# First layer, first MLP product: ten of fourteen tiles in five pairs, each pair as seven products of quarters

## The chip, the cores and the metric

The kernel runs on one core of one Trainium2 chip, in one launch. The metric is the device time of one execution in microseconds. An execution is a little longer than the span from its first to its last instruction, which the profile's times count from.

## What is computed

A vector `x` of 2048 tokens by 640 channels goes through two rounds of a spectral layer (A: a filter between a 2D FFT and its inverse) and a token-mixing MLP (B). B works across the tokens, for each channel alone:

```python
def _B_ref(x, w1, b1, w2, b2):
    h = _layernorm(x, axis=-1)                  # (B, S, D), S = 2048, D = 640
    u = jnp.einsum("bsd,sf->bdf", h, w1) + b1   # F = 1728
    u = _gelu(u)
    y = jnp.einsum("bdf,fs->bds", u, w2) + b2
    return (lambda x, *d: x.transpose(*d))(y, 0, 2, 1)   # (B, S, D)

x = x + _A_ref(_layernorm(x), A_w_r, A_w_i)
x = x + _B_ref(_layernorm(x), B_w1, B_b1, B_w2, B_b2)
x = x + _A_ref(_layernorm(x), A_w_r, A_w_i)
x = x + _B_ref(_layernorm(x), B_w1, B_b1, B_w2, B_b2)
```

The change concerns the einsum with `w1` in the first round.

## The kernel before

**Stages.** `run` calls, for each round, `a1` and `a2` (the spectral layer; `a2` ends with the normalised input `hf` of the MLP, 16 row blocks j of 128 tokens by 640 channels in f32) and then the MLP: `b1st` in the first round, `b2nd` in the second.

**Precision.** Every factor is split into a high and a low f16 part and a product is three matmuls (`mm3`): high x high, high x low, low x high. `hh` (or `hha` for rows 0 to 7, written already in `a2`) and `hl` are the parts of `hf`. Weights are scaled by a power of two first: `scan1` sums squares of a raw tile on ACT, `scale1` adds them on DVE, sums over the partitions by a one-column matmul with `ones` on PE, and takes the power on DVE in six small steps; `step(m)` advances this by one stage. `wload` fetches the raw f32 tile in two halves, `wsplit` makes the high part on ACT and the low part on DVE.

**The first product.** The 1728 columns of `w1` are 14 tiles of 128, the last one doubled to fill it (tile 13, whose two halves are added up afterwards). `SEQ` orders them in pairs t, t+7: 6, 13, 0, 7, 1, 8 and so on. A tile takes 16 row blocks x 3 terms x 2 halves of 320 channels, 96 matmuls (64 for tile 13). The first two tiles share the start: `both_high` runs their high parts against the rows that are there, the last four rows later, then `rest` adds the low rows. Each later tile is `both`, with the next tile's split and the scans of later tiles at fixed row blocks beside it. A gelu on ACT follows each tile; the split of its result into `uh` and `ul`, the factors of the second product, stands at the end.

**For the second round.** That round computes its first product by quarters: a pair of tiles is a 2 x 2 matrix of quarters A11 to A22 (first index the tile, second the half of the rows), `hf` one of B11 to B22, and seven products of sums (S1 to S4 of A, T1 to T4 of B) of 8 row blocks each take the place of eight. The first round forms the parts for it beside its own work and writes them to DRAM: `wstore` writes the split tiles, `wsum` forms S1 to S4 in buffers of their own, `wssplit` splits and writes them (pair 5's as f32 sums). All of these writes are issued by POOL.

**Order.** The tile framework orders instructions by readiness, except where `self.pin` is on: then `Pin` ties each instruction behind the one written before it on its engine. In `b1st` the pin is off for the copies of `hf` to `hh` (rows 8 to 15), on for the forming of `hl`, and off again for all that follows until the last three tiles. `a2` is pinned as a whole. DMA issues on SP go past `Pin`.

**The second product** (16 tiles of `w2`, 84 or fewer matmuls each, in the order of `SEQ`) follows at once, with its own splits and scans, and ends with the first steps of the second round's spectral layer. Its buffers (`a0_open`) lie where `h` and its neighbours were.

Of the kernel before, what the change touches and what calls it, by code (L numbers as in the profile page):

```python
# [3 lines left out]

# [6 lines left out]
F32 = mybir.dt.float32  # L11
# [41 lines left out]
SEQ = [t + 7 * i for t in (6, 0, 1, 2, 3, 4, 5) for i in range(2)]  # L53
# [34 lines left out]
class Layers:  # L88
# [41 lines left out]
    def setup(self):  # L130
# [16 lines left out]
        self.qt = base.tile([128, NFT], F32, name="qt")  # L147
        self.s2, self.c2 = (base.tile([128, NQ], F32, name=f"{a}p") for a in "sc")
        self.s1p, self.c1p, self.c1n = (base.tile([128, 7], F32, name=f"{a}p1") for a in "scn")
# [5 lines left out]
        self.second, self.nr = False, 4  # L155
# [70 lines left out]
    def scan1(self, m, cs=(0, 1)):  # L226
        if m < NFT + NJ:
            if 0 in cs:
                self.ssq = self.t(self.base, [128, 1, 2], F32, "sq", 2)
            for c in cs:  # L230
                self.scan(self.wraws[m][c], self.ssq[:, 0, c:c + 1])

    def scale1(self, m, at=None):

        V, (k, t, _) = self.V, self.wtile(m)
        c = slice(t, t + 1)
        q = self.t(self.base, [128, 1], F32, "q2", 2) if k else self.qt[:, c]
        for ps in self.total(self.ssq, at):
            yield
        V.tensor_scalar(q, ps, SMALL, WS ** -2, op0=ALU.max, op1=ALU.mult)  # L240
        i = self.pow2(q, self.st[k][:, c])
        V.tensor_scalar(self.ct[k][:, c], i, self.iu if k else 0.5 / ZS, None, op0=ALU.mult)
        yield
# [538 lines left out]
    def a2(self, li):  # L782
# [5 lines left out]
        if not first:  # L788
# [3 lines left out]
        q = 1 if first else 4  # L792
        self.hfa = [ph.tile([128, q, 2, 320], F32, name=f"hf{j}_{self.n}") for j in range(NJ // q)]
        self.hf = [self.hfa[j // q][:, j % q] for j in range(NJ)]
# [46 lines left out]
        if not first:  # L841
            V.tensor_tensor(self.c1p, self.ct[0][:, :7], self.ct[0][:, 7:], op=ALU.max)
            V.tensor_scalar(self.c1n, self.c1p, -1.0, None, op0=ALU.mult)
            V.tensor_tensor(self.s2, self.st[1][:, :NQ], self.st[1][:, NQ:], op=ALU.min)
            V.tensor_tensor(self.c2, self.ct[1][:, :NQ], self.ct[1][:, NQ:], op=ALU.max)
# [5 lines left out]
        for i in range(NJ + 5):  # L851
# [88 lines left out]
    def wload(self, m):  # L940
        k, t, n = self.wtile(m)
        src = self.A[("w2z" if self.second else "w2") if k else "w1"][t]
        raws = self.wraws[m] = []
        for c in (0, n // 2):
            raws.append(self.t(self.wr[max(m - 2, 0) % self.nr], [128, 8, 128], F32, "raw", 2)[:, :n // 2])
            self.nc.sync.dma_start(raws[-1], src[:, c:c + n // 2])
# [41 lines left out]
    def wsum(self, m, a):  # L988

        (a11, a12), (a21, a22) = self.wraws[m - 1], self.wraws[m]  # L990
        S = self.sums
        S[a] = self.t(self.pz, [128, 8, 128], F32, a, 1)
        x, y = {"S1": (a21, a22), "S3": (a11, a21), "S2": (S.get("S1"), a11), "S4": (S.get("S2"), a12)}[a]
        self.V.tensor_tensor(S[a], x, y, op=ALU.add)

    def wssplit(self, m, a):

        d = SEQ[m - 1]
        if d == 5:
            self.nc.gpsimd.dma_start(self.ws1[d][a], self.sums[a])  # L1000
            return
        s = self.s1p[:, d:d + 1]
        w = self.t(self.pz, [128, 2, 8, 128], F16, "sp", 2)
        self.T.activation(w[:, 0], self.sums[a], AF.Identity, scale=s)
        self.V.scalar_tensor_tensor(w[:, 1], self.sums[a], s, w[:, 0], op0=ALU.mult, op1=ALU.subtract)
        self.nc.gpsimd.dma_start(self.ws1[d][a], w)

    def b1st(self, li):
        nc, A = self.nc, self.A
        V, G, T = self.V, self.G, self.T  # L1010
        mm = self.PE.matmul
        ph = self.push("h", side=self.sq)
# [4 lines left out]
        sc = {m: self.scale1(m) for m in range(2, NFT + NJ)}  # L1017
        self.pin = True
        self.wsplit(1, (1,), hi=False)
        self.wload(2)  # L1020
        self.scan1(2)
        self.h = []
        for j in range(NJ):
            self.h.append((self.hh[j], ph.tile([128, 2, 320], F16, name=f"hl{j}_{self.n}")))
            V.tensor_tensor(self.h[j][1], self.hf[j], self.hh[j], op=ALU.subtract)
            if j == 9:
                next(sc[2])
        self.pin = False
        self.pop("hf")
        self.wr[1:] = (self.push(a, side=self.sp) for a in ("wr", "wr2", "wr3"))  # L1030
        pu = self.push("u", side=self.sp)
        uh = [pu.tile([128, 2, 320], F16, name=f"uh{f}_{self.n}") for f in range(NFT)]
        ul = [pu.tile([128, 2, 320], F16, name=f"ul{f}_{self.n}") for f in range(NFT)]
        pf = self.push("uf", side=self.sp)
        uf = [pf.tile([128, 2, 320], F32, name=f"uf{f}_{self.n}") for f in range(NFT)]
        p = self.pz = self.push("b1", side=self.sq)
        self.sums = {}
        for m in (3, 4, 5):
            self.wload(m)

        def ahead(m, w):
# [3 lines left out]
            self.wstore(m, w)  # L1045
# [8 lines left out]

        def step(m):
            if m in sc:
                next(sc[m])

        def usplit(ft, t):
            V.tensor_scalar(uh[ft], t, self.su, None, op0=ALU.mult)  # L1060
            c = slice(0 if ft < NFT - 1 else 64, 128)
            V.scalar_tensor_tensor(ul[ft][c], t[c], self.su[c], uh[ft][c], op0=ALU.mult, op1=ALU.subtract)
            if ft == NFT - 1:
                V.tensor_copy(ul[ft][:64], uh[ft][:64])
                G.memset(uh[ft][64:], 0.0)

        todo = iter(SEQ)

        def nextu():
            i = next(todo)  # L1070
            usplit(i, uf[i])

        def prod(ps, w, j, h, start=False, stop=False):
            for a in range(2):
                mm(ps[:, a, :320], w[:, j], h[:, a], start=start, stop=stop)

        def rest(ft, ps, w):
            for j in range(NJ):
                yield j
                prod(ps, w[0], j, self.h[j][1], stop=j == NJ - 1)  # L1080

        def both(ft, ps, w):
            for j in range(NJ):
                yield j
                prod(ps, w[0], j, self.h[j][0], start=j == 0)
                prod(ps, w[0], j, self.h[j][1])
                prod(ps, w[1], j, self.h[j][0], stop=j == NJ - 1)


        w = self.w.pop(0), self.w.pop(1)  # L1090
        pss = self.big(), self.big()
        self.both_high(pss, w, prod)
        for ft in range(NFT):
            if ft < 2:
                ps, run = pss[ft], rest(ft, pss[ft], w[ft])
                if ft:
                    self.wopen(2)
            else:
                ps = self.big()
                w2 = self.w.pop(ft)  # L1100
                run = both(ft, ps, w2)
                ahead(ft, w2)
            steps = prep(ft)
            for j in run:
                if ft % 2 and ft < NFT - 2 and 11 <= j < 15:
                    self.wsum(ft + 2, ("S1", "S3", "S2", "S4")[j - 11])
                if ft > 1:
                    m = ft + 1 - ft % 2
                    d = SEQ[m - 1]
                    if ft < m and j == 7:  # L1110
                        q = [self.st[0][:, t:t + 1] for t in (d, d + 7)]
                        V.tensor_tensor(self.s1p[:, d:d + 1], *q, op=ALU.min)
                    if j in ((9, 14) if ft < m else (1, 7)):
                        self.wssplit(m, {9: "S1", 14: "S2", 1: "S3", 7: "S4"}[j])
                if ft == 0:
                    if j in (8, 9):
                        step(2)
                elif ft == 1:
                    if j in (1, 2):
                        next(steps)  # L1120
                    if j in (8, 10):
                        self.scan1(3, (j // 2 - 4,))
                    if j == 15:
                        step(3)
                else:
                    if ft == 2 and j in (4, 5):
                        step(3)
                    if ft == 2 and j in (5, 6):
                        self.scan1(4, (j - 5,))
# [902 lines left out]
```

## Time and profile before

| | us |
|---|---|
| median of three runs | 988.71 (988.12 to 990.26) |
| the profiled execution | 989.59 |
| its span | 987.5 |
| start of `b1st` on PE to the third tile | 171.8 to 195.7 |
| third to fourteenth tile | 195.7 to 352.5 |

Rows of groups read: line, engine, operation, out<-in with shapes, count, busy time, mean ns of one, idle time before them and what ended it. Since a helper issues all instructions, they have one line (L80), and the names tell them apart. Rows of the timeline read: start, length, engine, line, operation, count, idle time before it and its releaser. PE's matmuls overlap: the distance of two starts is their cost, not the length.

### The profile page before, as it was taken

The page shows a single profiled execution, that of the slowest core. Times are in us where ns is not written, and L with a number is a line of the kernel's source. Part 1 is how long each engine was busy: PE and PEld are TensorE (multiplying, and loading weights), DVE is VectorE, ACT ScalarE, POOL GpSimd, SP SyncE. Part 2 cuts the span into 40 slices and gives each one's busy share as a digit, 9 for nine tenths or more (in the row PEclk, how much of TensorE's full clock was granted, in tenths as well). Part 3 has the DMA queues.
Part 4 walks back from the last instruction along what each step waited for, and adds up shares of the span by engine and source line. Part 5 has one row for each costly group of instructions (what it writes and reads, how often), then busy time and mean ns, then how long its engine had stood idle before and what let it go on. Part 6 is the DMA issues. An engine that isn't in the chain of part 4 may idle for free.

```text
span 987.5 us, 22744 instructions
## 1 busy us (share of the span) xinstructions
PE 950.2 (96%) x9134; PEld 705.8 (71%) x9134; DVE 734.6 (74%) x1430; ACT 546.3 (55%) x843; POOL 302.5 (31%) x516
## 2 busy tenths in 40 slices
PE   4889899999999999999999898999999999999998
PEld 3778777677777777777777676776777777777776
DVE  7979989986657765666666897889734455988885
ACT  5857869776555445555543476684433334454431
POOL 6949868322113102222222496672000000000000
PEclk9999999999999999999999999999999999999999
DMA  8856377667568564554411564674555447665411
GB/s 259 282 164 170 96 255 237 231 226 256 204 222 290 180 237 156 156 179 129 134 70 46 173 200 127 189 240 162 170 156 170 131 142 264 221 186 184 145 47 53
DMA packets 67485, 176.29 MB, mean 179 GB/s; under 512 B 8154, under 2 KB 15476, under 8 KB 67380
## 3 DMA queue, kind: packets, MB, share of 16 engines
q1 hardware_dynamic: 59380, 146.39, 46.5%
q0 software_dynamic: 8000, 28.46, 7.8%
q8 instruction: 71, 1.16, 0.5%
q14 instruction: 34, 0.28, 0.1%
HBM read 127.24 MB, written 47.58 MB: 177 GB/s over the span
## 4 chain that ended last, share of the span: by engine, by line
PE 78%; DVE 11%; POOL 5%; ACT 3%; issue 2%; DMA 1%; SPq 0%; POOLq 0%; DVEq 0%; ACTq 0%
PE ps L80 78%; DVE st L80 2%; DVE Yl L80 1%; DVE f L80 1%; DVE hl L80 1%; POOL xt L80 1%; DVE s1l L80 1%; DVE xt L80 1%; POOL xl L80 1%; POOL ta L80 1%; DVE tb L80 1%; ACT eh L80 1%; POOL eo L80 1%; DVE pl L80 1%; DVE ta L80 1%
## 5 line engine op out<-in xcount | busy, mean ns | idle before, releaser
L80 PEld LDWEIGHTS <-wh 128*128 128x128 f16 x2602 | 251.5, 98 | 100.5 <-issue 2.4
L80 PEld LDWEIGHTS <-wl 128*128 128x128 f16 x1610 | 157.5, 98 | 61.1
L80 PE MATMUL ps<-uh,wl 128*128 128x320 f16 x448 | 133.1, 299 | 0.0
L80 PE MATMUL ps<-ul,wh 128*128 128x320 f16 x448 | 133.1, 299 | 0.0
L80 PE MATMUL ps<-uh,wh 128*128 128x320 f16 x416 | 124.3, 299 | 0.0
L80 PE MATMUL ps<-hl,wh 128*128 128x320 f16 x496 | 102.2, 299 | 0.8 <-DVE hl L80 0.8
L80 DVE SCALAR_TENSOR_TENSOR wl<-raw,s,wh 128x896 f16<-128x896 f32 (+2 forms) x63 | 73.4, 1173 | 38.6 <-ACT wh L80 35.8
L80 PEld LDWEIGHTS <-wo 128*128 128x128 f16 x756 | 74.0, 98 | 28.7
L80 POOL TENSOR_TENSOR r<-v,mh 128x1 f32<-128x1 f32 x64 | 37.3, 583 | 158.3 <-DVE nm L80 149.1
L80 ACT ACTIVATE junk<-raw 128x896 bf16<-128x896 f32 (+1 forms) x60 | 59.5, 992 | 33.7 <-DMA raw<-w 29.2
L80 PE MATMUL ps<-tDi,Yh 128*128 128x322 f16 x320 | 72.7, 304 | 1.5 <-ACT Yh L80 1.5
L80 ACT ACTIVATE wh<-raw,s 128x896 f16<-128x896 f32 (+2 forms) x66 | 65.9, 1032 | 7.0 <-PE ps L80 5.2
L80 DVE TENSOR_TENSOR f<-eo 128x256 f32<-128x256 f32 (+1 forms) x124 | 40.9, 382 | 35.9 <-POOL eo L80 35.8
L80 POOL TENSOR_TENSOR xt<-xt,ec 128x320 f32<-128x320 f32 x64 | 53.2, 853 | 31.8 <-DVE xt L80 31.7
L80 DVE BATCH_NORM_STATS2 st<-xt 128x6 f32<-128x320 f32 x126 | 55.3, 481 | 5.2 <-DMA xt<-x 4.7
L80 PE MATMUL ps<-hha,wh 128*128 128x320 f16 x288 | 58.1, 299 | 0.9 <-DVE wh L80 0.9
L80 PE MATMUL ps<-u,wo 128*128 128x320 f16 x420 | 58.8, 299 | 0.0
L80 PE MATMUL ps<-tM,f 128*128 128x128 f32 x160 | 40.8, 436 | 18.5 <-DVE f L80 18.5
L80 PE MATMUL ps<-tDi,Yl 128*128 128x322 f16 x192 | 56.6, 303 | 1.4 <-DVE Yl L80 1.4
L80 POOL TENSOR_TENSOR eo<-z 128x320 f32<-128x320 f32 x60 | 52.2, 890 | 17.7 <-ACT z L80 15.4
L80 ACT ACTIVATE z<-xt,nb,r 128x640 f32<-128x640 f32 x31 | 28.5, 918 | 46.8 <-POOL z L80 38.2
L80 PE MATMUL ps<-hha,wl 128*128 128x320 f16 x256 | 53.3, 299 | 0.0
(248 smaller groups left out, 2253.1 us busy)
## 6 DMA issues: line engine op xcount, KB each, us to landing
xt<-x SPq DMA_DIRECT2D x79, 320.0 KB
raw<-w SPq DMA_DIRECT2D x32, 512.0 KB
w<-w SPq DMA_DIRECT2D x48, 321.0 KB
x<-xt SPq DMA_DIRECT2D x47, 320.0 KB
raw<-w SPq DMA_DIRECT2D x32, 448.0 KB
raw<-w2z SPq DMA_DIRECT2D x32, 448.0 KB
w1S<-sp POOLq DMA_DIRECT2D x20, 512.0 KB, 4.0
out<-xt SPq DMA_DIRECT2D x15, 320.0 KB
```

Source lines behind the costliest of these rows:

```text
L80: i = f(*a, **k)
```

## The change

Only `b1st`, what it shares with `b2nd`, and the loads ahead of it change.

The order becomes 6, 13, 5, 12, 0, 7, 1, 8, 2, 9, 3, 10, 4, 11. Tiles 6, 13, 5 and 12 stay whole (96, 64, 96 and 96 matmuls). The other five pairs are seven products each, A11, S1, S2, S4, S3, A12, A22, of 24 matmuls. The parts T1 to T4 are formed on DVE in place in `hf`, the sums S3 and S4 in place in the raw tiles, S1 and S2 in one buffer X. A pair has one scale, from the squares of both tiles. Pair 5's sums are formed on POOL. What was split for the first round is written for the second as it is. Evictions combine the seven products into four f32 quarters (on ACT, DVE and two adds on POOL), a gelu follows two quarters at a time, and `u` is laid out by pair. All of `b1st` up to the second product is written in one order with the pin on. Three raw tiles are loaded in `a2` already, by SP. The evictions of `b2nd` lose their negative factors, in the same number of instructions.

The diff, cut to its core (`halves` holds functions that stood in `b2nd` and are the same there):

```diff
-SEQ = [t + 7 * i for t in (6, 0, 1, 2, 3, 4, 5) for i in range(2)]
+SEQ = [t + 7 * i for t in (6, 5, 0, 1, 2, 3, 4) for i in range(2)]
+PAIR = 4
...
+            if first and i in (10, 13, 16):
+                self.wload({10: 2, 13: 3, 16: 5}[i])
...
     def b1st(self, li):
...
-        for j in range(NJ):
-            if j not in HA:
-                self.hh[j] = ph.tile([128, 2, 320], F16, name=f"hh{j}_{self.n}")
-                T.activation(self.hh[j], self.hf[j], AF.Copy)
...
         self.pin = True
...
+        def ssum(d, a, W):
+            if a == "S1":
+                X[d] = self.t(self.pX, [128, 8, 128], F32, "X", 1)
+            x, y, op = {"S1": ("A21", "A22", ADD), "S2": ("S1", "A11", SUB), "S3": ("A11", "A21", SUB), "S4": ("A12", "S2", SUB)}[a]
+            W.tensor_tensor(src(d, a), src(d, x), src(d, y), op=op)
+
+        def keep5(a):
+            ssum(5, a, G)
+            nc.gpsimd.dma_start(self.ws1[5][a], src(5, a))
...
+        places = [(self.wp[0], "wh"), (self.wp[0], "wl"), (self.px, "wo"), (self.wp[1], "wh"), (self.wp[1], "wl")]
+        def hi(n):
...
+                T.activation(wo[n][:, 0], src(d, a), AF.Identity, scale=self.s1p[:, d:d + 1])
+        def lo(n):
...
+                V.scalar_tensor_tensor(wo[n][:, 1], src(d, a), self.s1p[:, d:d + 1], wo[n][:, 0], op0=MUL, op1=SUB)
+                nc.gpsimd.dma_start(self.ws1[d][a], wo[n])
+        def product(n):
+            o = self.big()
+            bank[n], spot[0] = o[:, 0, :320], o[:, 1, 0:4]
+            for j in range(8):
+                self.mm3(bank[n], (wo[n][:, 0, j], wo[n][:, 1, j]), H.operand(PB[ops[n][1]], j), j == 0, j == 7)
...
+        def work(n, more=()):
+            evict(n - 1)
+            hi(n + 3)
+            d, k = (n + 4) // 7, (n + 4) % 7
+            a = {0: "S1", 1: "S3", 3: "S4"}.get(k)
+            if a and d < 5:
+                ssum(d, a, V)
+            lo(n + 3)
+            if k == 2 and d < 5:
+                ssum(d, "S2", V)
+            evicted(n - 1)
+            for e in more:
+                e()
...
+        for j in range(8, NJ):
+            T.activation(H.hhb[:, j - 8], self.hf[j], AF.Copy)
+        self.wsplit(1, (1,), hi=False)
+        self.wload(PAIR)
+        self.scan1(2)
+        self.scan1(3)
+        hlow(0)
+        hlow(1)
+        step(2)
...
+        prod(pss[0], w0[0], hhigh, early, start=True)
+        prod(pss[0], w0[1], hhigh, early)
+        step(2)
+        hlow(2)
+        step(2)
+        step(3)
+        keep5("S1")
+        prod(pss[1], w1[0], hhigh, early, start=True)
+        step(3)
+        self.scan1(4)
+        self.scan1(5)
+        hlow(3)
...
+        for i, q in ((0, w0[0]), (0, w0[1]), (1, w1[0])):
+            prod(pss[i], q, hhigh, late)
+        prod(pss[0], w0[0], hlows, every, stop=True)
...
+        tsum("T1", 0)
+        self.wsplit(2, (0,))
+        self.wsplit(2, (1,))
...
+        prod(pss[1], w1[0], hlows, every, stop=True)
+        tsum("T1", 1)
...
+        self.wsplit(3, (0,))
+        self.wsplit(3, (1,))
+        plain(1, sw, sw)
+        thi("T1")
+        step(4)
...
+        tlo("T1")
+        for a in "T2", "T3":
+            for c in range(2):
+                tsum(a, c)
+        thi("T2")
+        w = self.w.pop(2)
+        self.wstore(2, w)
+        for a in "S2", "S3", "S4":
+            keep5(a)
...
+        for d in range(1, 5):
+            a, b, n = 2 * d + PAIR, 2 * d + PAIR + 1, 7 * d
+            for k, (m, c) in enumerate(((a, 0), (b, 0), (a, 1), (b, 1))):
+                todo[max(n - 13 + k, -5)].append(lam(self.wload, m, (c,)))
+            for k, m, c in ((11, a, 0), (10, b, 0), (9, a, 1), (7, b, 1)):
+                todo[n - k].append(lam(self.scan1, m, (c,)))
+            for k in (6, 5):
+                todo[n - k].append(lam(step, a))
+        todo[-2] += [lam(tlo, "T2")]
+        todo[-1] += [lam(thi, "T3"), lam(tlo, "T3")]
+        todo[1] += [lam(tsum, "T4", 0), lam(tsum, "T4", 1)]
...
+        mms = {7 * d - 6: 2 * d + PAIR for d in range(1, 5)}
+        mms.update({27: a, 33: b})
...
+        for j in every:
+            if j % 4 == 0:
+                work(j // 4 - 4, todo[j // 4 - 4])
+            both(ps, w, j)
...
+        for n in range(len(ops)):
...
+            product(n)
+            work(n, todo[n])
+            if n in mms:
+                step(mms[n])
```

`ops` lists the 35 products in order; `work(n)` stands beside product n (n from -4 to -1 beside tile 12), `todo[n]` is what is added there, and `step(mms[n])` puts the one-column matmul of a scale behind product n on PE.

More of the change, by code (lines that the diff above doesn't have):

```diff
@@ L787, in a2 @@
         self.wp[1] = self.push("wb", side=self.sp)
-        if not first:
+        if first:
+            self.wr[1:] = (self.push(a, side=self.sp) for a in ("wr", "wr2", "wr3"))
+            self.px, self.pX = (self.push(a, side=self.sp) for a in ("px", "X"))
+        else:
             pu = self.push("u6", side=self.sp)
@@ new lines, in b1st, with step @@
+        hx = self.push("hx", side=self.sq)
+        H = self.halves(ph, pt, hx)
+        prod, tsum, thi, tlo, hlow, hhigh, hlows = H.prod, H.tsum, H.thi, H.tlo, H.hlow, H.hhigh, H.hlows
+        spot = [None]
+        sc = {m: self.scale1(m, at=lambda m=m: spot[0][:, m % 4:m % 4 + 1]) for m in range(2, NFT + 2)}
+        sc.update({m: self.scale1(m) for m in range(NFT + 2, NFT + NJ)})
+        self.pin = True
+        def step(m):
+            if m in sc:
+                next(sc[m])
+        R, X = {}, {}
@@ L1053, in prep @@
                 yield
[L1055 to L1087, printed above, removed]
```

422 lines of the change are left out of this document (217 added, 205 removed).

## The prediction

> **What bounds the kernel now.** I read the page first, then the stretches by stage, then the timeline of the first layer's MLP product, engine by engine.
>
> ```profile
> span 987.5 us, 22744 instructions
> PE 950.2 (96%) x9134; PEld 705.8 (71%) x9134; DVE 734.6 (74%) x1430; ACT 546.3 (55%) x843; POOL 302.5 (31%) x516
> 200.00:352.00 152.00, 152.00 (x1131) 109.49 (x1129) 105.99 (x197) 86.75 (x113) 31.01 (x59) 1.00 0.64 225
> 175.82 2.34 PE L80 MATMUL ps<-hha,wl 128*128 128x320 f16 x16
> 177.99 1.25 PE L80 MATMUL ps<-hh,wl 128*128 128x320 f16 x8
> 195.66 0.43 PE L80 MATMUL ps<-hha,wh 128*128 128x320 f16 x2
> 352.47 0.30 PE L80 MATMUL ps<-uh,wh 128*128 128x320 f16 x1
> ```
>
> The third row gives, after the stretch, its length and the busy time of PE, weight loads, DVE, ACT and POOL. PE is busy all 152 us at a granted clock of 1.00, the others at most 106 us: in this stage PE's instruction count is the time. Sixteen matmuls take 177.99 - 175.82 = 2.17 us, 0.1357 us each (the 2.34 holds the drain of the last). The third tile (tile 5 after the change) starts at 195.66, the second product at 352.47. Those two times are what I recompute.
>
> **What the change takes away.** A tile costs 16 x 3 x 2 = 96 matmuls, a pair 192; a pair as seven products costs 7 x 8 x 3 = 168. Five pairs lose 5 x 24 = 120 matmuls, 120 x 0.1357 = **-16.3 us**, all of it on the path. A product is 24 matmuls, 3.26 us. The second layer runs the same scheme already, without the forming of parts beside it, so the saving itself needs no guess.
>
> **What it moves at the head.** Before, the copies hf to hh of rows 8 to 15 and the first matmuls are written while the pin is off, and were woven into the end of `a2`. After, they are written with the pin on: each goes behind everything written earlier for its engine. For ACT that is the last normalised row.
>
> ```profile
> 174.71 1.36 ACT L80 ACTIVATE hh<-hf 128x640 f16<-128x640 f32 x2
> 178.19 0.92 ACT L80 ACTIVATE hf<-xt,nb,r 128x640 f32<-128x640 f32 x1 [0.54 <-POOL nb L80]
> 180.86 0.92 ACT L80 ACTIVATE hf<-xt,nb,r 128x640 f32<-128x640 f32 x1 [0.97 <-POOL nb L80]
> 181.81 0.74 ACT L80 ACTIVATE hh<-hf 128x640 f16<-128x640 f32 x1
> 182.45 1.04 ACT L80 ACTIVATE junk<-raw 128x1024 bf16<-128x1024 f32 x1
> 184.79 1.28 ACT L80 ACT_TABLE_LOAD   x1
> 174.73 1.25 PE L80 MATMUL ps<-hh,wh 128*128 128x320 f16 x8
> 191.05 0.15 DVE L80 TENSOR_SCALAR qt<-ps 128x1 f32<-128x1 f32 x1
> 191.98 0.15 DVE L80 TENSOR_SCALAR c<-qi 128x1 f32<-128x1 f32 x1
> L80 DVE TENSOR_TENSOR hlb<-hf,hhb 128x2560 f16<-128x2560 f32 x2 | 5.5, 2812 | 0.0
> ```
>
> The last row `hf` ends at 181.8 (it waits for POOL, not for the copies, so freeing ACT of them hardly moves it). Two copies take 1.36, so eight run 181.8 to 187.2: row 8 is there at 182.5, row 11 at 184.5. PE has done the first eight rows (16 matmuls) by 176.2 and then, in order, waits for row 8; before, it ran rows 8 to 11 at 174.73. Row 11 leaves PE at 184.9, the 24 matmuls with the low weights end at 188.1. The next instruction on PE is the one that sums the squares of tile 5 for its scale. Its two scans stand on ACT behind the copies: 187.2 + (184.79 - 182.45) = 189.5, plus DVE's sum, 189.8. Then 24 matmuls to 193.1. The next such sum waits on DVE, which has `hlow` (2.8) and the scale's six small steps (191.05 to 192.13, 1.1) between: 193.8. Then 24 + 64 matmuls, 11.9: the third tile starts at 205.8 instead of 195.66, **+10.1 us**. With the 16 matmuls done at 176.2 nothing else is queued on PE to fill this; DVE and ACT have nothing late behind it that would cost more.
>
> **What it adds between the third tile and the products.** Durations of what is new there:
>
> ```profile
> L80 DVE TENSOR_TENSOR hf<-hf 128x1280 f32<-128x1280 f32 x4 | 5.8, 1479 | 0.0
> L80 DVE TENSOR_TENSOR T2l<-hf,T2h 128x1280 f16<-128x1280 f32 x2 | 2.9, 1480 | 0.0
> L80 ACT ACTIVATE T2h<-hf 128x1280 f16<-128x1280 f32 x2 | 2.5, 1272 | 0.3
> L80 DVE TENSOR_TENSOR S<-raw,raw 128x1024 f32<-128x1024 f32 x12 | 14.5, 1219 | 0.1
> L80 DVE SCALAR_TENSOR_TENSOR wl<-raw,s,wh 128x1024 f16<-128x1024 f32 x25 | 31.6, 1282 | 27.3 <-ACT wh L80 24.7 <-DMA w1S<-sp 2.6
> L80 ACT ACTIVATE sp<-S,sp 128x1024 f16<-128x1024 f32 x20 | 22.5, 1142 | 15.3 <-DVE sp L80 10.3 <-DMA w1S<-sp 4.8
> L80 ACT ACTIVATE junk<-raw 128x1024 bf16<-128x1024 f32 x28 | 29.5, 1052 | 26.1 <-DMA raw<-w 25.8
> L80 POOL TENSOR_TENSOR xt<-xt,ec 128x320 f32<-128x320 f32 x32 | 25.9, 810 | 31.8 <-DVE xt L80 31.7
> L80 POOL TENSOR_TENSOR xl<-ta,xh 128x642 f16<-128x642 f32 x30 | 42.4, 1419 | 5.1 <-ACT xh L80 5.0
> L1006 POOL DMA_DIRECT2D w1S<-sp x20 | 10.7, 535 | 38.0 <-DVE sp L80 32.5 <-DVE s L80 2.7 <-DVE qi L80 2.1
> 196.86 1.41 ACT L80 ACTIVATE sw<-ps 64x640 f32<-64x640 f32 x2
> w1fS<-S POOLq DMA_DIRECT2D x4, 512.0 KB, 5.8
> 244.34 0.33 SPq L946 DMA_DIRECT2D raw<-w  x1
> 250.58 1.06 ACT L80 ACTIVATE junk<-raw 128x1024 bf16<-128x1024 f32 x1 [1.89 <-DMA raw<-w]
> ```
>
> PE runs tiles 5 and 12 (192 matmuls, 26.1) to 231.9 and products 0 and 1 to 238.4. What must be ready then is the sum of squares for pair 1: its matmul is written behind product 1 on PE, and its DVE half behind the low part of product 4's weights. So all of DVE's list up to there counts. Tile 12's weights are split when tile 13 has left PE: 205.8, drain 0.3, two copies on ACT 1.4, high part 1.1, low part of the first half 1.3: 209.9. Behind that DVE has the second half 1.3, a scale 1.25, two T1 lows 3.0, four T sums 5.9, S1 and S3 of pair 0 2.4, to 223.7. Then it needs the high part of product 0 from ACT, and ACT stands in front of a scan of pair 1's first raw half. That half reuses the buffer of tile 5's A11, which now holds S4 of pair 5, formed on POOL. No POOL sum of 1024 columns is in the trace; 320 take 0.81 and 642 take 1.42, so by their slope 2.1 (ends: 1.4, the longest seen, and 2.6, 3.2 times the 320). S3 begins when tile 12's first half is split, 209.9; two sums and two issues (0.54 each) end at 215.2. The write lands 5.8 later in the median, about 221; the load then takes about as long as the quoted one, 250.58 - 244.34 = 6.2, less where the queue is emptier, I take 5.4. So the raw half is there at about **226.5**, and ACT has stood idle from 220.5 (tile 5 leaves PE at 218.8, its gelu follows).
>
> From the landing: scan 1.2 and high part 1.1 on ACT; then on DVE 1.3 (low 0), 1.0 waiting behind the next scan, 1.3 (low 1), 1.2 (S2), 3.0 (T2 low), 1.2 (S4), 1.3 (low 2), 3.0 (T3 low), 1.3, 1.3 and the sum 0.2: 18.4, so 244.9. PE stands **6.5 us** before product 2. If the load landed by 220.5, DVE's list alone would end at 239 and the stall would be 0.5; landing at 228 makes it 8. These are its ends.
>
> Idle PE costs clock as well:
>
> ```profile
> 608.00:612.00 4.00, 1.79 (x35) 1.12 (x36) 3.62 (x10) 2.45 (x6) 1.14 (x8) 0.99 0.47 129
> 612.00:614.00 2.00, 2.00 (x9) 1.07 (x9) 0.00 (x0) 0.00 (x0) 0.00 (x0) 0.50 0.05 12
> 614.00:616.00 2.00, 2.00 (x11) 1.25 (x10) 0.00 (x0) 0.31 (x1) 0.00 (x0) 0.66 0.00 0
> 616.00:618.00 2.00, 2.00 (x17) 1.51 (x16) 1.40 (x2) 0.54 (x2) 0.00 (x0) 1.00 0.00 0
> ```
>
> PE was busy 1.79 of 4 us, and the next 2 + 1.4 us ran at 0.50: 1.7 us lost. A 6.5 us gap should bring the same, **+1.7 us** (ends 0 and 3.4, none or two such stretches) after the second gap. At the head it falls on matmuls that then wait for the scan (188.1 against 189.8), so there I count nothing. The Trainium skill, "TensorE: Matmul & The Clock Gate", section "What's actually happening", says the clock halves after one idle window of about 3.4 us and returns after one busy window; by that rule too this change, whose gaps exceed a window, loses about 1.7 us a gap, and the quoted rows agree (3.4 us at half).
>
> **What it adds beside the products, at nothing or nearly.** Per pair of 22.8 us DVE gets seven low parts (9.0), four sums (4.9), five evictions and a scale:
>
> ```profile
> L80 DVE SCALAR_TENSOR_TENSOR f<-ps,c,f 128x320 f32<-128x320 f32 x12 | 6.6, 547 | 9.5 <-PE ps L80 9.5
> L80 ACT ACTIVATE f<-ps,b1s,cp 128x320 f32<-128x320 f32 x6 | 3.6, 608 | 0.0
> L80 DVE SCALAR_TENSOR_TENSOR u<-f,su,u 128x1280 f16<-128x1280 f32 x5 | 7.8, 1551 | 7.3 <-ACT u L80 7.3
> 150.00:160.00 10.00, 10.00 (x72) 7.54 (x71) 9.53 (x30) 9.57 (x16) 8.13 (x15) 1.00 0.88 290
> 40.00:44.00 4.00, 3.29 (x13) 2.91 (x13) 3.93 (x15) 3.77 (x11) 3.66 (x10) 1.00 0.98 352
> ```
>
> 5 x 0.55 + 1.3 make it 17.9. ACT: 8.0 + 4 scans 4.8 + two evictions 1.2 + two gelus 1.8 = 15.8. Both fit, and parts are formed three products ahead, so PE covers them; without that cover a late step would cost its 1.3. Thin is only the matmul for the next pair's scale at products 8, 15 and 22: behind the product's start stand ACT's eviction 0.6 and high part 1.1, DVE's low part 1.3 and sum 0.2, together 3.2 against 3.26 of product. With hand-overs I count 0.2 each there and at 27 and 33, **+0.8 us** in all (ends 0 and 3). The parts' writes (35 of 512 KB instead of 20 and the tiles') move the same bytes. The raw loads moved into `a2` meet a stage that moves 290 GB/s at most, against 352 seen elsewhere: nothing. U's split makes DVE's step 0.55 + 1.28 + 1.55 = 3.4 in some of the products from 28 on, 0.1 over; the parts' lead of three products covers that. The second product's first row of x lands on a wait that exists before too.
>
> **The sum.** The terms are -16.3 + 10.1 + 6.5 + 1.7 + 0.8 = +2.8. Laid along the timeline (244.9, 33 products 107.5, clock 1.7, thin places 0.8) the second product starts at 354.9 instead of 352.47, **+2.4 us**; the 0.4 between them is what before's stage holds beside its full matmuls. I take +2.4. The profiled execution took 989.59, so 992.0 there; the median shown is 988.71, 0.9 less, so **991.1 us**. A measurement of this kernel tells about 0.2%, 2 us, from no change.
>
> **The rivals.** (1) The raw half lands in time. Then the second gap and its clock go: 991.1 - 6.5 - 1.7 = **982.9**. For it: the median landing comes from a crowded stage. Against: two POOL sums, a write and a load stand in one row, and no faster step is in the trace. (2) The copies do not wait for the end of `a2`, so the head costs nothing: 991.1 - 10.1 = **981.0**, and 973 with (1). Against: the pin is written ahead of the loop. (3) Slower: the thin place decides. A pair's scale is late by x whenever the raw halves of the pair land over 4 us later than planned, since each is loaded only when the part formed in its buffer two pairs earlier is done; ACT's scan then holds back the eviction and high part behind it. At 3 us for each of three pairs: **1000**. For it: scans waited 25.8 us for loads already, in the row above. Against: the plan leaves three products, 9.8 us, for a load of some 6.
>
> **How the numbers follow.** Forecast 0.48, (1) 0.23, (2) 0.12, (3) 0.13, 0.04 for what I don't see. The forecast's own range by its ends (stall 0.5 to 8, clock 0 to 3.4, thin places 0 to 3) is 986 to 996. The whole range reaches to (1), (2) alone and most of (3): 980 to 998. Slower by over 2 us: 0.27 of the forecast, (3), 0.02 more, 0.42. Within: 0.16 of it, 0.04 of (1), 0.02 more, 0.22. Faster: 0.36.
>
> **What would show it.** PE idle some 6 us in front of the first `hhb` matmul, then until the third tile about 10 us behind the time of before; a second gap ahead of product 2, released by DVE's `sqb`, with ACT's scan waiting for a raw half earlier; the clock at 0.50 behind it; 24 matmuls of 3.26 us everywhere else. Wrong if `hhb` is copied before the last `hf`, or if PE goes from product 1 to product 2 without a gap.

## The result, and the profile after

The changed kernel takes 1000.04 us in the median of 4 runs (996.44 to 1002.54), the kernel before 989.37 beside it (988.12 to 990.26): ratio 1.0106, 95% interval 1.0066 to 1.0146. It is slower by 10.7 us; the forecast was 991.1, range 980 to 998. The page's head, then PE's rows of the timeline (start, length, engine, line, operation, count, idle time before it and its releaser):

```profile
span 1000.5 us, 22481 instructions
PE 942.2 (94%) x9009; PEld 697.2 (70%) x9009; DVE 758.1 (76%) x1392; ACT 563.8 (56%) x864; POOL 325.9 (33%) x515
```

```profile
122.40 0.43 PE L83 MATMUL ps<-tDi,Yh 128*128 128x322 f16 x2 [0.31 <-ACT Yh L83]
178.71 2.35 PE L83 MATMUL ps<-hha,wh 128*128 128x320 f16 x16
188.91 2.57 PE L83 MATMUL ps<-hhb,wh 128*128 128x320 f16 x8 [7.85 <-ACT hhb L83]
211.51 0.43 PE L83 MATMUL ps<-hha,wh 128*128 128x320 f16 x2
246.22 0.16 PE L83 MATMUL ps<-sqb,ones 128*128 128x1 bf16 x1 [1.94 <-DVE sqb L83]
271.65 0.16 PE L83 MATMUL ps<-sqb,ones 128*128 128x1 bf16 x1 [2.44 <-DVE sqb L83]
336.89 0.16 PE L83 MATMUL ps<-sqb,ones 128*128 128x1 bf16 x1 [1.39 <-DVE sqb L83]
359.76 0.43 PE L83 MATMUL ps<-u,wh 128*128 128x320 f16 x2
367.27 0.16 PE L83 MATMUL ps<-sqb,ones 128*128 128x1 bf16 x1 [3.27 <-DVE sqb L83]
```

PE is busy 8 us less than before (950.2) and the span is 13.0 us longer: the saving is there, and PE waits for more than it saves. The rows cut the span at the same points as before's. The last two columns are a second profile of the changed kernel (`c_after`, below) and of the fastest kernel of this study (`e10_best`). The first row's start is that of `a2`; its end is the start of the matmuls with rows 0 to 7 (178.71), of which the kernel before has eleven, 1.5 us, already inside `a2`. Counted by equal work, `a2` loses 1.5 us more than the rows below say, and the head 1.5 us less.

| stretch on PE, us | before | after | again | `e10_best` |
|---|---|---|---|---|
| up to `a2` | 120.35 | 122.40 | 120.53 | 120.60 |
| `a2` | 53.69 | 56.31 | 54.90 | 52.90 |
| head: from there to the third tile | 21.62 | 32.80 | 32.79 | 25.97 |
| third tile to the second product | 156.81 | 148.25 | 148.23 | 142.51 |
| second product | 189.31 | 194.42 | 194.43 | 191.67 |

The forecast had 0, 0, +10.1, -7.7 and 0 in these rows; they came out +2.05, +2.62, +11.18, -8.56 and +5.11, and in the second profile +0.18, +1.21, +11.17, -8.58 and +5.12. The head and the products came out within 1.1 us of the sum; for the products that is luck, since two errors inside cancel (see below). The loss that was not foreseen lies on both sides of them.

**The head** in the timeline, all engines:

```profile
184.34 7.85 DVE L83 TENSOR_TENSOR hl<-hf,hha 128x1280 f16<-128x1280 f32 x4
184.93 2.35 POOL L83 TENSOR_SCALAR nb<-mv,r 128x1 f32<-128x1 f32 x1
187.24 3.60 POOL L83 TENSOR_TENSOR X<-raw,raw 128x1024 f32<-128x1024 f32 x1
187.31 0.92 ACT L83 ACTIVATE hf<-xt,nb,r 128x640 f32<-128x640 f32 x1 [3.07 <-POOL nb L83]
188.14 5.11 ACT L83 ACTIVATE hhb<-hf 128x640 f16<-128x640 f32 x8
```

The copies stand behind the last `hf`, and that waits for POOL, whose `nb`, one column, takes 2.35 us beside DVE's lows. The windows (length, then busy time of PE, weight loads, DVE, ACT and POOL, then granted clock, DMA share and GB/s) show the clock:

```profile
184.00:186.00 2.00, 0.00 (x0) 0.00 (x0) 2.00 (x3) 0.24 (x1) 1.90 (x2) 0.56 0.44 52
192.00:194.00 2.00, 2.00 (x10) 1.08 (x8) 0.19 (x1) 2.00 (x3) 0.00 (x0) 0.50 0.64 262
194.00:196.00 2.00, 2.00 (x15) 1.35 (x14) 0.50 (x2) 1.94 (x5) 0.00 (x0) 0.88 0.00 0
```

From 184.2 to 194.4 PE is at half clock: it stands still until 188.9 and then runs slowly while the scans of tile 5 end. No idle time is left in front of their sum.

**`a2`.** The window of before, then that of after at the same place of the stage, and two rows of its timeline:

```profile
140.00:150.00 10.00, 10.00 (x74) 7.68 (x72) 8.82 (x22) 9.53 (x16) 7.38 (x12) 1.00 0.76 257
```

```profile
142.00:152.00 10.00, 8.84 (x63) 6.68 (x62) 6.99 (x17) 7.76 (x14) 6.02 (x10) 1.00 0.99 387
```

```profile
150.35 1.06 ACT L83 ACTIVATE junk<-raw 128x1024 bf16<-128x1024 f32 x1 [2.04 <-DMA raw<-w]
161.82 0.89 DVE L83 TENSOR_TENSOR xt<-xt,ps 128x320 f32<-128x320 f32 x2 [1.17 <-DMA xt<-x]
```

Written at rows 10, 13 and 16, the raw loads went out as soon as their buffers were free (from 103 and from 127 us) and filled the DMA engines (share 0.99), and a scan and an x row of `a2` came late.

**The second product's start:**

```profile
363.56 0.55 DVE L83 SCALAR_TENSOR_TENSOR f<-ps,cp,f 128x320 f32<-128x320 f32 x1
364.42 0.81 ACT L83 ACTIVATE f<-f,b1s 128x640 f32<-128x640 f32 x1
365.27 0.83 ACT L83 ACTIVATE u<-f,su 128x640 f16<-128x640 f32 x1
366.00 0.94 ACT L83 ACTIVATE junk<-raw 128x896 bf16<-128x896 f32 x1
367.06 0.16 DVE L83 TENSOR_REDUCE sqb<-sqFalse 128x1 bf16<-128x2 f32 x1
```

The rows are the last eviction, the last gelu, the last part of U (its high half), and then the last scan of the second product's third tile, which is pinned on ACT behind them, with the sum of it on DVE. PE meets its sum 4.2 us after the start (367.27 - 3.27 - 359.76) and waits 3.27 us; then the clock is at half from 368.5 to 371.9, 1.7 us more.

### The profile page after: what moved, and what is told of

It is laid out like the page before. It is cut to its first block, busy times and chain, and to the rows that moved or that the text cites. A ratio compares the mean times of both kernels' runs of the same rounds, so it can differ in the third digit from the quotient of the medians.

```text
span 1000.5 us, 22481 instructions
## 1 busy us (share of the span) xinstructions
PE 942.2 (94%) x9009; PEld 697.2 (70%) x9009; DVE 758.1 (76%) x1392; ACT 563.8 (56%) x864; POOL 325.9 (33%) x515
## 4 chain that ended last, share of the span: by engine, by line
PE 50%; DVE 7%; ACT 3%; POOL 3%; issue 2%; DMA 2%; SPq 0%; DVEq 0%; ACTq 0%; POOLq 0%
PE ps L83 50%; DMA raw<-w2z 1%; DVE xt L83 1%; DVE u L83 1%; DVE wl L83 1%; POOL ta L83 1%; POOL xl L83 1%; DVE st L83 1%; DVE S L83 1%; POOL xt L83 1%; ACT eh L83 1%; DMA w<-w 0%; DVE wh L83 0%; DMA stk<-rest 0%; ACT xh L83 0%
## 5 line engine op out<-in xcount | busy, mean ns | idle before, releaser
L83 PEld LDWEIGHTS <-wh 128*128 128x128 f16 x2298 | 223.2, 98 | 99.5 <-issue 11.6
L83 PE MATMUL ps<-u,wh 128*128 128x320 f16 x1242 | 233.3, 300 | 0.2 <-DVE wh L83 0.2
L83 PEld LDWEIGHTS <-wl 128*128 128x128 f16 x1626 | 160.4, 99 | 70.2 <-issue 6.1
L83 PE MATMUL ps<-u,wl 128*128 128x320 f16 x826 | 186.8, 300 | 0.0
L83 PEld LDWEIGHTS <-wo 128*128 128x128 f16 x924 | 90.3, 98 | 37.2 <-issue 2.1
L83 POOL TENSOR_TENSOR eo<-z 128x320 f32<-128x320 f32 x60 | 52.4, 894 | 17.4 <-ACT z L83 15.7
L83 DVE SCALAR_TENSOR_TENSOR wl<-raw,s,wh 128x896 f16<-128x896 f32 (+2 forms) x43 | 48.7, 1138 | 11.0 <-ACT wh L83 10.8
L83 PE MATMUL ps<-hhb,wh 128*128 128x320 f16 x224 | 46.0, 304 | 8.3 <-ACT hhb L83 8.2
L83 PEld LDWEIGHTS ps<-tM,f 128*128 128x128 f32 x160 | 33.1, 297 | 25.4 <-DVE f L83 25.0
L83 ACT ACTIVATE wh<-raw,s 128x896 f16<-128x896 f32 (+2 forms) x46 | 43.5, 988 | 9.1 <-PE ps L83 7.6
L83 POOL MEMSET wl<- 64x256 f16 x2 | 0.6, 307 | 146.6 <-DMA wl<-w2A 146.6
L83 POOL TENSOR_TENSOR xl<-ta,xh 128x642 f16<-128x642 f32 (+2 forms) x34 | 45.5, 1346 | 5.9 <-ACT xh L83 5.9
```

What stands on the lines that cost most here:

```text
L83: i = f(*a, **k)
```

## The experiments

Each is the changed kernel with the edit shown. Times are medians; ratios are against the kernel before on the same chip.

**e1_copies: the copies unpinned.**

```diff
+        self.pin = False
         for j in range(8, NJ):
             T.activation(H.hhb[:, j - 8], self.hf[j], AF.Copy)
+        self.pin = True
```

> The eight copies of hf to hhb are written with the pin off, so that they may go between the last normalised rows on ACT; nothing else is changed. Theory: they set the first wait of the head (7.85 us in front of the first hhb matmul at 188.91) and push the scans of tile 5 to 193.2. Then PE has rows 0 to 11 done by about 186 and waits only for the sum of squares, whose scans begin when the last hf ends (188.2): sum at about 191 instead of 196.1, third tile near 206.4 instead of 211.5, 5 us gained of 1000. Rival: the last normalised row and POOL's late nb (2.35 us) set the head by themselves, and the copies stand in their shadow: third tile earlier by under 1 us, time within 1 us.

995.39 us, ratio 1.0046 (1.0029 to 1.0063). PE's timeline of this run:

```profile
176.96 2.35 PE L83 MATMUL ps<-hha,wh 128*128 128x320 f16 x16
179.15 1.25 PE L83 MATMUL ps<-hhb,wh 128*128 128x320 f16 x8
190.56 0.19 PE L83 MATMUL ps<-sqb,ones 128*128 128x1 bf16 x1 [6.90 <-DVE sqb L83]
```

Row 8 is there in time and the wait moves to the sum of tile 5. The third tile starts at 208.32, 31.36 us into the head instead of 32.80: 1.4 us, not 5. The half clock moved along with the wait (188.8 to 195.7), and of the missing 3.6 us 2.6 are lost in its part behind 190.56. Neither theory had the size.

**e5_head: the copies unpinned and the two scale matmuls out of the way too** (the edit above, and:)

```diff
         prod(pss[0], w0[1], hhigh, early)
-        step(2)
-        hlow(2)
-        step(2)
-        step(3)
-        keep5("S1")
         prod(pss[1], w1[0], hhigh, early, start=True)
...
+        hlow(2)
+        hlow(3)
         for i, q in ((0, w0[0]), (0, w0[1]), (1, w1[0])):
             prod(pss[i], q, hhigh, late)
+        step(2)
+        step(2)
+        step(3)
...
         prod(pss[0], w0[0], hlows, every, stop=True)
+        step(3)
```

> Copies with the pin off as in the run before, and on PE the two one-column matmuls of tiles 5 and 12 go behind the matmuls that wait for neither (all 96 with high rows, and the 32 with tile 6's low rows); on DVE the lows of rows 8 to 15 come ahead of the steps of these scales. Theory: freeing the copies alone gained 1.4 us at the head because the wait moved to the sum of tile 5 (6.9 us in front of it); with that matmul out of the way PE has 9.8 us of work after a2 and then needs the last rows, the third tile starts some 24.5 us after a2's last matmul instead of 32.8, 8 us gained. Rival: the lows on DVE (done 200 us in the profile of the changed kernel) hold PE next: 3 us gained.

991.85 us, 1.0013 (1.0002 to 1.0024). The head takes 27.62 us, 5.2 less than in the changed kernel. What is left:

```profile
196.68 1.25 PE L83 MATMUL ps<-hlb,wh 128*128 128x320 f16 x8 [1.49 <-DVE hlb L83]
199.22 0.16 PE L83 MATMUL ps<-sqb,ones 128*128 128x1 bf16 x1 [1.29 <-DVE sqb L83]
```

Theory and rival each hold a part: the order on PE and ACT is worth 5.2 us, and behind it stand DVE's lows.

**e6_hl: DVE's lows later.**

```diff
+        step(2)
         hlow(0)
         hlow(1)
-        step(2)
```

> The first four lows on DVE (hl of rows 0 to 7) are written behind the sum of tile 5's squares instead of ahead of it; nothing else. Theory: they slow POOL down while they run (nb 2.35 us instead of 0.27 or 0.55, the sum X 3.60) and that delays the last row of hf. Moved away, nb takes under 0.6, X 2.6 or less, the last hf ends 1.8 us earlier after a2's end, and with it the copies, scans and the third tile: 1.8 us gained. Rival: POOL's times do not depend on DVE: nb stays at 2.35, and the lows, now late, hold PE: 1 to 3 us lost.

1004.41 us, 1.0143 (1.0124 to 1.0162): slower. POOL, DVE and PE in its timeline:

```profile
183.96 0.27 POOL L83 TENSOR_SCALAR nb<-mv,r 128x1 f32<-128x1 f32 x1
184.19 2.35 POOL L83 TENSOR_TENSOR X<-raw,raw 128x1024 f32<-128x1024 f32 x1
192.52 5.70 DVE L83 TENSOR_TENSOR hl<-hf,hha 128x1280 f16<-128x1280 f32 x4
202.08 0.16 PE L83 MATMUL ps<-sqb,ones 128*128 128x1 bf16 x1 [5.97 <-DVE sqb L83]
```

Apart, both engines are faster: `nb` 0.27 instead of 2.35, the sum X 2.35 instead of 3.60, the four lows 5.70 instead of 7.85. PE gets row 8 2.1 us sooner (8.10 us into the head, not 10.20). But the lows, begun 9 us later in the head, now hold back the second sum, and the head takes 38.94 us. The mechanism is shown; its cure by this edit costs more than it saves.

**e2_loads and e7_loads2: the raw loads in `a2` held back.** First all six behind SP's writes of rows 8, 11 and 14, then only the last four, behind row 14 (the diff is that of the second):

```diff
+            done = nc.sync.dma_start(self.xs[li + 1][i - 2], xt[i - 2][:, :D])
...
-            if first and i in (10, 13, 16):
-                self.wload({10: 2, 13: 3, 16: 5}[i])
+            if first and i == 10:
+                self.wload(2)
+            if first and i == 16:
+                with self.after(done):
+                    self.wload(3)
+                    self.wload(5)
```

> The six raw loads that stand in a2 are issued behind SP's writes of rows 8, 11 and 14 instead of ahead of a2's own loads; the instructions of all other queues stay as they are. Theory: issued at 103 and 127 to 142 us they fill the DMA engines (share 0.99 from 142 to 152) and delay a2's scan of the next weights by 2.0 us and its x rows by 1.2; held back, a2 on PE (first tDi matmul to the hha matmuls) takes 53.7 us again instead of 56.3: 2.6 us gained. If the two loads at 103 us also cause the 1.9 us gap of PE at 112.5 and its clock, another 2 us go, 4.7 in all. Rival: a2 is late for another reason (the gaps follow the start of a2, which is late by 2 us already): a2 stays at 56 us and the time within 1 us.

> Of the six raw loads in a2 the two of the first tile stay free (they go out at 103 us), and the other four go behind SP's write of row 14. Theory: the delay in a2 comes from loads issued while a2's own loads are in flight; with none from 127 to 165 us a2 takes 53.7 us on PE as in the kernel before, 1.1 to 2.6 us less than in the four profiles with early loads, and nothing new waits, since these tiles are needed from 187 us on. Rival: they are late there (POOL's sum X, the scans): what a2 gains the head loses, time within 1 us.

e2_loads: 1000.68 us, 1.0099 (1.0073 to 1.0125): no gain; `a2` takes 55.40, with one gap of 1.46 us at 167.69 behind an x row that now waits 2.2 us, and the clock is at half from 174.4 to 177.8, across its end at 175.18. e7_loads2: 994.57 us, 1.0046 (1.0031 to 1.0061); `a2` takes 53.01 and PE has no gap in the windows where it had them:

```profile
140.00:150.00 10.00, 10.00 (x73) 7.68 (x72) 8.99 (x23) 9.77 (x17) 7.60 (x14) 1.00 0.77 264
150.00:160.00 10.00, 10.00 (x73) 7.67 (x72) 9.62 (x29) 9.43 (x15) 8.07 (x14) 1.00 0.86 293
```

Over all profiles of the changed kernel and its variants, `a2` took 54.8 to 57.3 us in the eight with the early loads and 52.9 to 53.0 in the four that hold four back to row 14, where they go out behind its end on PE (in e7_loads2 at 174.39, the end is at 172.77). So raw loads issued within this stage, which itself loads, cost it 2 to 4 us, early (before 143 us) as late (155.59 and 167.34 in e2_loads).

**c_after: the changed kernel again.**

> The changed kernel once more, for its spread. In the profiles so far a2 starts on PE between 119.8 and 122.4 us with the same instructions ahead of it, so the 2.05 us by which it started later than in the kernel before are taken for chance, not for the early loads. Theory: another profile of the same kernel starts a2 near 120 to 121 and ends 1 to 2 us earlier, median 998 to 1000. Rival: the loads at 103 us delay the end of the first stage each time: a2 starts after 122 again.

998.46 us (998.04 to 999.99), 1.0086 (1.0063 to 1.0109). `a2` starts at 120.53 with the same two loads at 103 us, as the theory had it: the 2.05 us in the first profile are not the loads' doing but chance. The change costs 8.5 us by these runs and 10.7 by the first, with intervals that overlap.

**e3_scales: each later scale matmul one product later.**

```diff
-            for k in (6, 5):
+            for k in (6, 4):
                 todo[n - k].append(lam(step, a))
...
-        mms = {7 * d - 6: 2 * d + PAIR for d in range(1, 5)}
-        mms.update({27: a, 33: b})
+        mms = {7 * d - 5: 2 * d + PAIR for d in range(1, 5)}
+        mms.update({28: a, 33: b})
```

> The one-column matmul of each later scale, and the DVE steps that use it, stand one product later; the sum of squares on DVE stays where it is. Theory: PE's gaps at products 2 (1.94 us), 8 (2.44 and 1.7 of clock) and 27 (1.39) are all waits of that one matmul for DVE, which is behind by up to one product there; one product (3.26 us) of room takes all three away: 7 us gained. Rival: DVE's lag is a real shortage; the next thing that PE needs from DVE (the low part of a product's weights) is then late in its place, and 2 us or less are gained.

993.44 us, 1.0027 (1.0009 to 1.0045). Third tile to second product takes 143.76 us, 4.5 less. The gaps at 2 and 27 are gone; two are left, at product 9 and, new, at 33, whose matmul had not been moved:

```profile
268.99 0.16 PE L83 MATMUL ps<-sqb,ones 128*128 128x1 bf16 x1 [1.27 <-DVE sqb L83]
349.33 0.16 PE L83 MATMUL ps<-sqb,ones 128*128 128x1 bf16 x1 [1.84 <-DVE sqb L83]
```

The waits were waits of that matmul, and one product of room is not quite enough in the first pair.

**e9_nosum: three of POOL's sums left out.**

```diff
         def keep5(a):
-            ssum(5, a, G)
+            if a == "S1":
+                ssum(5, a, G)
```

> Leaves out three of the four sums of pair 5 that POOL forms in the changed kernel (S2, S3, S4; the unsummed buffers are written instead), so the second round's pair 5 is not that of the reference. Theory: the gap ahead of product 2 (1.94 us) is the end of DVE's list, and DVE is slow there because POOL's sums run beside it (T1 low 2.52 each instead of 1.48, the pair's scale 1.30 instead of 0.15): without them DVE is 3 us ahead and the gap goes, though no raw half is waited for in either kernel; 2 us gained, and up to 2 more at product 8. Rival, the step on record: the scan of pair 1's first raw half waits for the load behind S4's write; then that scan starts earlier than 17.4 us after the third tile's start, and DVE's operations keep their lengths.

DVE's row in the changed kernel, with POOL, SP and ACT beside it and its sum for product 2 last, and then in this run:

```profile
219.06 5.04 DVE L83 TENSOR_TENSOR T1l<-hf,T1h 128x1280 f16<-128x1280 f32 x2
220.19 2.57 POOL L83 TENSOR_TENSOR raw<-raw,X 128x1024 f32<-128x1024 f32 x1
222.78 1.66 SPq L958 DMA_DIRECT2D raw<-w  x2
228.89 1.04 ACT L83 ACTIVATE junk<-raw 128x1024 bf16<-128x1024 f32 x1
246.01 0.15 DVE L83 TENSOR_REDUCE sqb<-sqTrue 128x1 bf16<-128x4 f32 x1
```

```profile
218.32 0.15 DVE L83 TENSOR_TENSOR sp<-s 128x1 f32<-128x1 f32 x1
218.39 2.89 DVE L83 TENSOR_TENSOR T1l<-hf,T1h 128x1280 f16<-128x1280 f32 x2
```

The gap ahead of product 2 is gone; that at product 8 stays (2.37 us). The scan starts 14.0 us after the third tile instead of 17.4, because ACT is free sooner, and waits for no load in either kernel; DVE's lengths did change (its two T1 lows take 2.89 instead of 5.04). In the changed kernel DVE works from 216.83 to 246.16 without a pause. So the gap was DVE's list, made longer by POOL, and not the raw half. The time, 998.79 us, 1.0088 (1.0065 to 1.0111), shows no gain over c_after: what its profile gains in the products (146.09 us, 2.1 less, with 3.4 us at half behind product 8 in both) it loses in `a2` (57.25). The cause is shown, its worth in time is not.

**e4_second: the second product's scale matmul 24 matmuls later.**

```diff
-                if i in (6, 7):
+                if i in ((14, 15) if j == 0 else (6, 7)):
                     step(m + 2)
```

> In the first tile of the second product the one-column matmul for the third tile's scale stands 24 matmuls later; nothing else. Theory: that matmul alone makes the 3.27 us gap at 367.3 and the half clock of 1.7 us behind it, since its last scan stands on ACT behind the last gelu and the last split of u: 5 us gained. Rival: PE waits there for the last parts of u, which are ready at the same time (367.0): the gap only moves, under 1 us gained.

994.24 us, 1.0043 (1.0028 to 1.0059). The second product takes 191.40 us, 3.0 less:

```profile
362.64 0.16 PE L83 MATMUL ps<-sqb,ones 128*128 128x1 bf16 x1 [1.93 <-DVE sqb L83]
```

1.3 us of the gap and all of the half clock behind it are gone; the second may be chance, since in e8_all a gap of 2.01 us ahead of the same matmul has 3.4 us at half behind it. PE reaches the matmul 5.6 us after the start instead of 4.2, since the scheduler had already put it later than written; the sum is later still.

**e8_all, e10_best, e11_adds: the parts together.** e5_head, e7_loads2 and e3_scales (with product 33's matmul moved too); for the second product, e8_all puts the scan ahead of the last gelu, and e10_best moves only the matmul, by 42 (`(20, 21)` in the place of `(14, 15)`). e11_adds is e10_best with `V` for `G` in the two additions of `evict`.

> All four together: the head as in e5_head, the loads as in e7_loads2, the later scales one product later (that of product 33 too), and in the second product's first tile the third scale's scan ahead of the last gelu and its matmul 24 matmuls later. Theory: the terms add: 8 at the head, 6 at the products, 5 in the second product, 1 to 2.6 in a2, so 978 to 981 us, faster than both kernels. Rival: DVE, with no gap of PE's left to catch up in, is short by 2 to 4 us in the first pair (23.8 us of work with the forming of T4 against 22.8 of products) and becomes the wait there: 983 to 986.

> e8_all with the second product's change put differently: scan and steps on ACT and DVE as in the changed kernel, the third scale's matmul 42 matmuls later. Theory: in e8_all the scan ahead of the last gelu made that gelu, and the last split, later (gaps of 0.83 and 2.01 us and 1.7 of clock); with only PE's matmul moved, and far enough, none is left: 977. Rival: the last low part of u holds PE by itself: 980 to 982.

> e10_best with POOL's two additions a pair (128x320, into the quarters) done by DVE. Theory: on POOL they take 1.47 and slow two operations of DVE beside them by 0.55 to 0.6 each; on DVE two of about 0.45 cost less than that, so the gap at product 9 (1.76) shrinks and the last pair's end (two additions of POOL in 5.17 us) too: 1 to 2 us below e10_best. Rival: DVE is the shorter-handed engine there and the additions lengthen its list: 1 to 2 us above e10_best.

981.52 us, 0.9913 (0.9899 to 0.9928); 981.50, 0.9920 (0.9892 to 0.9947); 982.41, 0.9919 (0.9891 to 0.9946). All three are faster than the kernel before, and not told apart. e8_all gains 17.6 us on c_after (each against the kernel before beside it), where the parts were expected to add to 20 to 21.6. In the profiles e10_best gains 2.5 us on e8_all in the second product (191.67 against 194.16), which its median doesn't show; e11_adds shortens the gap at product 9 from 1.76 to 1.08 and lengthens the one at the second product's start from 0.82 to 1.39. What PE still waits for in e10_best from the products to the second product's first tile, in the view of waits (total, times, longest):

```profile
PE ps L83 <- DVE sqb L83: 3.0, 2, 1.8
PE ps L83 <- DVE wl L83: 0.8, 1, 0.8
```

## Why the prediction was wrong

The forecast was +2.4 us, the runs show +8.5 and +10.7. Two steps that were put at nothing make up most of the difference, the raw loads in `a2` and the second product's start; two terms inside the stage were mis-sized in opposite directions.

**The saving, -16.3: right.** In e10_best the stretch from the third tile to the second product is 142.51 us with one gap of 1.76: 140.75 against 156.81, 16.06 less.

**The head, +10.1: right in its steps, +11.2 measured.** Last `hf`, then copies, row 8, then the sum of tile 5. What was not in it is POOL's `nb` under DVE's lows. The half clock took the place of the wait for the sum, as the prediction had it, so it cost under 0.5 of its own there (the sum is formed at 195.66, PE takes it at 196.10); it did cost the remedy in e1_copies. By equal work (the eleven matmuls in `a2` before) the head lost 9.7. The second rival fails here: the copies did wait for the last `hf`.

**The second gap, 6.5 and 1.7: mis-sized, 1.94 and 0 measured.** The step that failed is "that half reuses the buffer of tile 5's A11, which now holds S4". SP's load goes out at 222.78, when POOL's last sum, S4, has read A12 (220.19 + 2.57 = 222.76), and the write of S4 is only issued at 223.06: the half has A12's buffer, and no write to DRAM stands in the chain. The first rival's condition, the half in time, was met, but a gap stays: the prediction put it at 0.5 if DVE's list alone decides, and beside POOL's sums that list makes it 1.94, as e9_nosum shows. The clock's 1.7 is a matter of chance: none behind this gap in the two profiles of the changed kernel, 3.4 us at half in e1_copies, e4_second, e6_hl and e7_loads2, where the products are the same. There the wait at product 8 is 0.76 instead of 2.44, and the stretch takes 146.6 us instead of 148.2.

**The thin places, 0.8: mis-sized, 3.83 of gaps and 1.7 of clock.** The list of what stands "behind the product's start" began with ACT's eviction. At product 8 DVE is a product behind (the low parts, the forming of T4, and POOL's additions beside it; of these only the additions were tried, and e11_adds takes 0.7 off the gap, while e9_nosum leaves it without POOL's sums), and the list begins earlier. DVE and ACT of the changed kernel:

```profile
266.32 0.54 DVE L83 SCALAR_TENSOR_TENSOR f<-ps,cp,f 128x320 f32<-128x320 f32 x1
266.90 0.83 ACT L83 ACTIVATE f<-f,b1s 128x640 f32<-128x640 f32 x1 [0.29 <-DVE f L83]
267.63 1.04 ACT L83 ACTIVATE junk<-raw 128x1024 bf16<-128x1024 f32 x1
269.08 1.14 ACT L83 ACTIVATE wl<-raw,sp 128x1024 f16<-128x1024 f32 x1
270.25 1.28 DVE L83 SCALAR_TENSOR_TENSOR wl<-raw,sp,wl 128x1024 f16<-128x1024 f32 x1 [2.19 <-ACT wl L83]
271.45 0.15 DVE L83 TENSOR_REDUCE sqb<-sqTrue 128x1 bf16<-128x4 f32 x1
```

The first pair's last eviction comes 0.66 us after product 8 has started (265.66), and gelu, scan, ACT's eviction, high and low part follow it one by one to 271.45. The third rival has this chain, with another start: none of it waits for a load. That its 1000 is also the measured time is chance: it cost 2.44 and 1.7 at one pair, not 3 at each of three. At product 27 (1.39) DVE's own list ends late, with the sum at 336.70; what made it late was not tried.

The second gap was put 6.3 us too high (8.2 against 1.94) and the thin places 4.7 too low (0.8 against 5.5). That these nearly cancel is why the stretch came out at -8.6 against -7.7: luck, not a right account.

**"The raw loads moved into `a2` ...: nothing": wrong**, +1.2 and +2.6 in the two profiles, +2.7 and +4.1 by equal work; e7_loads2 takes 1.9 and 3.3 of it back. The bound was a rate, 290 against 352 GB/s, and forgot that loads written at row 10 leave when their buffers are free, ahead of `a2`'s own.

**The largest miss is what the sum left out, +5.1** (3.27 of waiting, 1.7 of clock). It ended at the second product's start. "U's split ... the parts' lead of three products covers that" holds for the products, and behind the last of them there is no lead: last eviction, gelu, U's split and the third tile's scan are one chain on DVE and ACT. e4_second and e10_best take back 3.0 and 2.8 us by moving the one-column matmul that waits for the end of this chain to a later place on PE.

With the terms put right (0.2, 1.2, 11.2, -8.6, 5.1) the second profile's sum is +9.1, against 8.5 in its median.

## What to carry to other kernels

A saving on the bounding engine has to be followed past the stage in which it is made, to the first place where that engine again waits for the others: here the tail cost 5 us that no row of the stage shows. Where a whole stage is pinned, a single small instruction on PE (a one-column matmul for a scale) carries the wait of a long chain on two other engines; moving it later gained 4.5 us in the products (e3_scales) and 3.0 in the second product (e4_second), with the chain left as it was. A load without an order of its own goes where the buffer lets it, so its place in the code did not tell what it collided with.

## What was not expected of the hardware

**POOL and DVE slow each other.** A one-column operation of POOL took 2.35 us beside DVE's 1280-column subtractions and 0.27 without them; a sum of 1024 columns 3.60 against 2.35; DVE's subtractions 1.96 (7.85 / 4) against 1.43 (5.70 / 4), and beside POOL's sums 2.52 (5.04 / 2) against 1.45 (2.89 / 2). The Trainium skill, "GPSIMD Engine Reference", section "Key points", says that the two share their interfaces to SBUF and contend when DVE reads two inputs from there. All these operations of DVE do, and the runs agree.

**The same gap costs clock in one run and none in the next.** Windows of PE behind the gap ahead of product 2, 1.94 us in the changed kernel and 1.95 (at 243.03) in e1_copies:

```profile
246.40:249.80 3.40, 3.40 (x27) 2.45 (x26) 3.40 (x3) 3.38 (x4) 0.52 (x1) 1.00 0.95 290
```

```profile
243.40:246.80 3.40, 3.40 (x15) 1.96 (x14) 3.40 (x3) 3.40 (x4) 0.33 (x1) 0.50 0.91 316
```

The same holds for longer ones: behind the gap of 2.44 at 271.65 the changed kernel has 3.4 us at half, behind one of 2.43 at 265.25 e5_head has none. And e5_head has 3.4 us at half behind its two gaps at the head, while e10_best, with the same two, has none; their heads differ by 1.65 us. So 1.7 us more or less in a stretch of one profile need not come from the edit. The Trainium skill, "TensorE: Matmul & The Clock Gate", section "What's actually happening", has a window of about 3.4 us that runs freely, and a clock that halves after an idle one. The stretches of 3.4 us agree with it, and so does the head, at half from 184.2 to 194.4, 10.2 us or three such windows, with PE idle in the first and until 188.9 in the second. A window that runs freely also fits that the same gap costs clock in one run only. But gaps of 1.95, 2.44 and 3.27 us, shorter than a window, were enough here, and the measurement decides. How much idle time it takes no run shows.
